# A retention and two MLP layers on one core: decay factors spread by TensorE, masks shared with ScalarE, weight conversion cut into pieces

## The chip, the cores and the metric

The kernel runs on one core of a Trainium2 chip. The metric is the device time of one execution in microseconds (us), the median of repeated runs; lower is better.

## What is computed

```
gamma[h] = 1 - 2**(-5 - h)                      # 8 heads, 2 batches, 768 steps, head size 64
state = gamma * state + outer(k[t], v[t])
y[t]  = (1/sqrt(64)) * q[t] @ state
x = y as 1536 tokens x 512
h = x @ w_in;  x = (h * sigmoid(h)) @ w_out     # layer 0: 512 -> 2048 -> 512
h = x @ w_in;  out = max(0.01 * h, h) @ w_out   # layer 1: 512 -> 2048 -> 512
```

Everything is float32 at the borders of the kernel. The weights arrive as 64-bit words of eight bytes each, which the kernel turns into float32 itself.

## The kernel before, in words

**Retention, in 12 chunks.** The sequence is cut into chunks of 128 steps, six for each of the two batches, taken in turns (`ORDER`); the loop over `j` runs over them. A chunk has a tile pair `att_t` of two halves of 512 KB: half 0 has the queries and keys with features on the rows, half 1 the values and keys with tokens on the rows. There are four such pairs, so the load of chunk j + 4 waits until chunk j has been read. The loads all stand on SP's queue (`load_att`, L104), with the first weight loads (`load_w`, L112) between them.

For chunk j TensorE does, in this order:
- `scores(j)` (L193): keys times queries, into one of two PSUM pairs
- `values(j)`: values times the masked scores `P` (L212), then the carried state times the queries (L221, not in a batch's first chunk), then the addition `u` to the state (L230, not in a batch's last chunk)

`scores(j + 1)` is issued ahead of `values(j)`. VectorE does `masked(j)` (L200: `P` = scores times mask `M`), `store_x(j)` (the output is split into a rounded part `xh`, copied by ScalarE at L255, and a remainder `xl`, L256) and `state(j)` (L241, L243). GpSimd (POOL) does `queries(j)` (L169: queries times the decay factors `G`, in place), `keys(j)` (L175) and `decay(j)` (L182).

The decay factors `G` (128 rows x 512) scale the output. For the first LATE = 4 chunks VectorE multiplies the finished product by `G` (L251) inside `store_x`; from chunk 4 on POOL multiplies the queries, before `scores` may read them. `G` comes by a load of its own (L361), the sixth on SP's queue. The masks `M`, one for each of the 8 heads, are made by VectorE (L366) from one mask and a column of factors that both arrive with the small load `cs` (L344).

**Weights.** A weight tile of 128 x 512 words goes through five steps: the load into `ws` (three buffers), `words` on ScalarE (L130, L131: two activations into `r` and `u`, two buffers of each), `conv` on VectorE (L137, L141, L145, L149, four instructions in a row), and `split_w` (a rounded copy by ScalarE, L154, and the remainder by VectorE, L155). `keep_w` (L116) then stores the pair to a scratch, from which later sets of tokens fetch it. The first six weights are `early`. Weights 0 and 1 are converted within the retention (at j = 5 and j = 9), 2 and 3 right behind it.

**The MLP layers.** The 1536 tokens are three sets of 512. `up` (L269) makes one of 16 blocks of 128 hidden features for one set, 12 matmuls into PSUM bank 3 or 2 in turns; `act` (L281, L283) reads that bank twice on ScalarE, which frees it, and VectorE makes the remainder (L284, called `rest`); `down` (L297) adds the block into four banks. For sets 0 and 1 the list `ops` goes up, up, down, over and over. Each engine works its instructions in the order in which the loop over `ops` issues them: at step i the conversion (`conv`) of the weight that step i + SPLIT = i + 5 needs, then `act` of step i - 1, then `words` for step i + 6, then the remainder, then `split_w`:

```
            for w in at(i + SPLIT, is_new):
                conv(w)
            done = i and ops[i - 1][1] == 0
            if done:
                rest = act(*ops[i - 1][:1], *ops[i - 1][2:])
            for w in at(i + SPLIT + 1, is_new):
                words(w)
            if done:
                rest()
            for w in at(i + SPLIT, is_new):
                split_w(w)
```

Of the kernel before, what the change touches and what calls it, by code (L numbers as in the profile page):

```python
# [9 lines left out]
F32 = mybir.dt.float32  # L10
# [4 lines left out]
AF = mybir.ActivationFunctionType  # L15
ALU = mybir.AluOpType
# [12 lines left out]
CS = T // C  # L29
ORDER = [b * NC + c for c in range(NC) for b in range(B)]  # L30
WARM = 18
LATE = 4
LAG = 2
SPLIT = 5
FETCH = 5
# [9 lines left out]
def retention_moe_kernel(ctx: ExitStack, tc: tile.TileContext, att, w1, w2, cst, out):  # L45
# [84 lines left out]
        nc.scalar.activation(out=r.bitcast(F32), in_=t[:, :, 1].bitcast(F32), func=AF.Abs)  # L130
        nc.scalar.activation(out=u, in_=t[:, :, 0].bitcast(U32), func=AF.Copy, scale=2.0 ** -29)  # L131

    def conv(w):
        t = stage.pop(w)
        r, u = rs[w]

        nc.vector.tensor_scalar(  # L137
            out=r.bitcast(F32), in0=r.bitcast(F32), scalar1=MIN_NORMAL, scalar2=MAX_NORMAL,
            op0=ALU.max, op1=ALU.min,
        )  # L140
        nc.vector.tensor_scalar(  # L141
            out=r, in0=r, scalar1=3, scalar2=0x3FFFFFF8,
            op0=ALU.logical_shift_left, op1=ALU.bitwise_and,
        )
        nc.vector.scalar_tensor_tensor(  # L145
            out=r, in0=t[:, :, 1], scalar=-0x40000000, in1=r, op0=ALU.bitwise_and, op1=ALU.bitwise_or
        )

        nc.vector.tensor_tensor(out=r, in0=r, in1=u, op=ALU.add)  # L149

    def split_w(w):
        r = rs.pop(w)[0].bitcast(F32)
# [189 lines left out]

    with tc.manual_schedule():
        nc.scalar.dma_start(out=cs, in_=cst[:, 0:ncs])  # L344
        z = gp.tile([128, 256], BF, tag="gf", name="z")
        nc.vector.memset(z, 0.0)
        warm = bank(3)
        for i in range(WARM):
            nc.tensor.matmul(out=warm[:, 0:256], lhsT=z[:, 0:128], rhs=z, start=True, stop=True)

        z1 = gp.tile([128, 1], F32, tag="gf", name="z1")
        nc.vector.memset(z1, 0.0)
        nc.scalar.activation(out=z1, in_=z1, func=AF.Silu)

        early = [weight[i] for i in range(SPLIT + 4) if new[i]]
        load_att(0, 0)
        load_att(1, 0)
        load_att(0, 1)
        load_att(2, 0)
        load_att(1, 1)  # L360
        nc.sync.dma_start(out=G, in_=cst[:, ncs:])  # L361
        load_att(3, 0)
        load_att(2, 1)
        load_att(3, 1)
        for h in range(H):
            nc.vector.tensor_scalar(  # L366
                out=M[:, h % 2, (h // 2) * C:(h // 2) * C + C], in0=mask, scalar1=MD[:, h:h + 1],
                scalar2=None, op0=ALU.mult,
            )
        NJ = len(ORDER)  # L370
        scores(0)
        masked(0, 2)
        for j in range(NJ):
            if j + 1 < NJ:
                queries(j + 1)
                scores(j + 1)
            keys(j)
            decay(j)
            values(j)
            if j + 4 < NJ:  # L380
                load_att(j + 4, 0, 1)

            if j in (1, 3, 5, 6, 10):
                load_w(early[(1, 3, 5, 6, 10).index(j)])
            w = early[(5, 9).index(j)] if j in (5, 9) else None
            if w:
                words(w)
            if j == NJ - 2:
                words(early[2])
            if j + 1 < NJ:  # L390
                masked(j + 1)
            if w:
                conv(w)
            store_x(j)
            state(j)
            if w:
                split_w(w)
            if j in (7, 11):
                keep_w(early[(7, 11).index(j)])
        conv(early[2])  # L400
        split_w(early[2])
        words(early[3])
        load_w(early[5])
        keep_w(early[2])
        widen()

        for i, op in enumerate(ops):
            l, p, b, f = op
            if i >= len(ops) - LAST:
                break  # L410
            for w in at(i + SPLIT + 4, is_new):
                if w not in early:
                    load_w(w)
            for w in at(i + SPLIT - 1, is_new):
                if w not in early[:3]:
                    keep_w(w)
            for w in at(i + FETCH, is_old):
                fetch_w(w)
            if p == 0:
                up(l, b, f)  # L420
            else:
                for m in range(4):
                    down(m, l, b, f)
                    if f == NF - 1:
                        finish(m, l, b, f)
                free.append(gt.pop((l, b, f)))
            if not kept[i]:
                free.append(W.pop(weight[i]))
# [6 lines that stand above are left out]
                words(w)  # L435
            if done:
                rest()
            for w in at(i + SPLIT, is_new):
                split_w(w)
        for m in range(4):  # L440
            for l, p, b, f in ops[-LAST:]:
                down(m, l, b, f)
            finish(m, l, b, f)
# [47 lines left out]
```

## Time and profile before

| what | value |
|---|---|
| median of 3 runs | 587.32 us (585.93 to 587.69) |
| the profiled execution: its time, its span | 586.51 us, 584.7 us |
| TensorE busy | 570.3 us (98% of the span) |
| VectorE, ScalarE, POOL busy | 285.3 us (49%), 234.6 us (40%), 25.9 us (4%) |
| retention: first to last matmul of it | 5.12 to 52.95 us |
| mean granted TensorE clock | 0.997 |

The span is the time from the first to the last instruction of the profiled execution; 1.8 us of its own time lie around it. A share of busy time is a mean over stages: TensorE is busy almost throughout, and what it waits for lies in the first 63 us.

### The profile page before, as it was taken

The page shows a single profiled execution, that of the slowest core. Times are in us where ns is not written, and L with a number is a line of the kernel's source. Part 1 is how long each engine was busy: PE and PEld are TensorE (multiplying, and loading weights), DVE is VectorE, ACT ScalarE, POOL GpSimd, SP SyncE. Part 2 cuts the span into 40 slices and gives each one's busy share as a digit, 9 for nine tenths or more (in the row PEclk, how much of TensorE's full clock was granted, in tenths as well). Part 3 has the DMA queues.
Part 4 walks back from the last instruction along what each step waited for, and adds up shares of the span by engine and source line. Part 5 has one row for each costly group of instructions (what it writes and reads, how often), then busy time and mean ns, then how long its engine had stood idle before and what let it go on. Part 6 is the DMA issues. An engine that isn't in the chain of part 4 may idle for free.

```text
span 584.7 us, 8034 instructions
## 1 busy us (share of the span) xinstructions
PE 570.3 (98%) x3026; PEld 472.0 (81%) x3026; DVE 285.3 (49%) x477; ACT 234.6 (40%) x422; POOL 25.9 (4%) x30
## 2 busy tenths in 40 slices
PE   7899799999999999999999999999999999999997
PEld 6787688888888888888888888888888888888885
DVE  4777888888883311134975635776661111110000
ACT  1223766766663322144655434555452312213001
POOL 2860000000000000000000000000000000000000
PEclk9999899999999999999999999999999999999999
DMA  8994777777758855718598777798876965562901
GB/s 323 344 340 161 262 235 266 240 265 241 259 187 295 296 200 186 275 46 306 203 360 305 282 254 261 238 336 296 286 252 236 370 208 194 189 207 82 384 3 72
DMA packets 40071, 142.43 MB, mean 244 GB/s; under 512 B 4448, under 2 KB 4576, under 8 KB 40032
## 3 DMA queue, kind: packets, MB, share of 16 engines
q1 hardware_dynamic: 39744, 141.58, 68.4%
q8 instruction: 24, 0.39, 0.3%
q10 hardware_dynamic: 288, 0.34, 0.2%
q14 instruction: 15, 0.12, 0.1%
HBM read 105.20 MB, written 36.70 MB: 243 GB/s over the span
## 4 chain that ended last, share of the span: by engine, by line
PE 92%; DVE 3%; DMA 3%; ACT 1%; issue 0%; POOL 0%; SPq 0%; DVEq 0%; ACTq 0%; POOLq 0%
PE b L269 44%; PE p L297 22%; PE b L297 22%; DMA G<-cst_dram 1%; DMA att_t<-att_dram 1%; PE b L212 1%; PE b L221 1%; PE p L193 1%; DVE P L200 1%; POOL att_t L169 0%; SPq L104 0%; PE b L230 0%; DVE r L141 0%; DVE r L145 0%; DVE xl L256 0%
## 5 line engine op out<-in xcount | busy, mean ns | idle before, releaser
L269 PE MATMUL b<-xh,s 128*128 128x512 f32 x560 | 183.0, 392 | 3.4 <-ACT s L281 3.4
L269 PEld LDWEIGHTS b<-xh,s 128*128 128x128 f32 x560 | 106.0, 189 | 26.1 <-ACT s L281 3.8
L284 DVE TENSOR_TENSOR s<-gf,s 128x512 fp32r<-128x512 f32 x73 | 50.4, 691 | 142.0 <-ACT s L283 94.6
L269 PE MATMUL b<-xl,s 128*128 128x512 f32 x280 | 109.5, 391 | 0.0
L297 PE MATMUL b<-s,s 128*128 128x512 f32 x288 | 73.1, 389 | 0.0
L297 PE MATMUL p<-s,s 128*128 128x512 f32 x288 | 73.1, 389 | 0.0
L283 ACT ACTIVATE gf<-b 128x512 f32<-128x512 f32 x48 | 28.6, 596 | 103.0 <-PE b L269 103.0
L269 PE MATMUL b<-xh,sr 128*128 128x512 f32 x208 | 67.8, 389 | 0.0
L297 PEld LDWEIGHTS b<-s,s 128*128 128x128 f32 x288 | 54.1, 188 | 11.2
L297 PEld LDWEIGHTS p<-s,s 128*128 128x128 f32 x288 | 54.1, 188 | 11.2
L269 PEld LDWEIGHTS b<-xl,s 128*128 128x128 f32 x280 | 53.0, 189 | 10.9
L281 ACT ACTIVATE gf<-b 128x512 f32<-128x512 f32 x48 | 28.3, 590 | 62.9 <-PE b L269 62.7
L154 ACT ACTIVATE s<-r 128x512 fp32r<-128x512 f32 x46 | 29.1, 633 | 59.3 <-DVE r L149 59.3
L149 DVE CUSTOM_DVE_ANT_0 r<-r,u 128x1024 uint16<-128x1024 uint16 x64 | 44.3, 692 | 7.2
L269 PEld LDWEIGHTS b<-xh,sr 128*128 128x128 f32 x208 | 39.1, 188 | 8.1
L145 DVE SCALAR_TENSOR_TENSOR r<-ws,r 128x512 int32<-128x512 int32 x64 | 44.3, 693 | 2.2
L130 ACT ACTIVATE r<-ws 128x512 f32<-128x512 f32 x64 | 43.1, 674 | 2.0 <-DMA ws<-w_dram 2.0
L131 ACT ACTIVATE u<-ws 128x512 int32<-128x512 uint32 x64 | 43.3, 677 | 0.0
L269 PE MATMUL b<-xl,sr 128*128 128x512 f32 x104 | 40.5, 389 | 0.0
L155 DVE TENSOR_TENSOR s<-r,s 128x512 fp32r<-128x512 f32 x46 | 31.8, 690 | 16.1 <-ACT s L154 14.7
L284 DVE TENSOR_TENSOR sr<-gf,sr 128x512 fp32r<-128x512 f32 x23 | 15.9, 691 | 41.9 <-ACT sr L283 21.1
L297 PE MATMUL b<-sr,s 128*128 128x512 f32 x120 | 30.4, 389 | 0.0
(56 smaller groups left out, 557.0 us busy)
## 6 DMA issues: line engine op xcount, KB each, us to landing
s<-scr SPq DMA_DIRECT2D x71, 512.0 KB, 4.5
ws<-w_dram SPq DMA_DIRECT2D x64, 512.0 KB, 4.9
scr<-s SPq DMA_DIRECT2D x46, 512.0 KB, 3.1
sr<-scr SPq DMA_DIRECT2D x41, 512.0 KB, 4.4
att_t<-att_dram SPq DMA_DIRECT2D x24, 512.0 KB, 7.3
scr<-sr SPq DMA_DIRECT2D x18, 512.0 KB, 3.0
out_dram<-ob SPq DMA_DIRECT2D x11, 256.0 KB, 2.1
G<-cst_dram SPq DMA_DIRECT2D x1, 256.0 KB, 7.8
```

The lines of the kernel that those rows point to most:

```text
L130: nc.scalar.activation(out=r.bitcast(F32), in_=t[:, :, 1].bitcast(F32), func=AF.Abs)
L131: nc.scalar.activation(out=u, in_=t[:, :, 0].bitcast(U32), func=AF.Copy, scale=2.0 ** -29)
L145: nc.vector.scalar_tensor_tensor(out=r, in0=t[:, :, 1], scalar=-0x40000000, in1=r, op0=ALU.bitwise_and, op1=ALU.bitwise_or)
L149: nc.vector.tensor_tensor(out=r, in0=r, in1=u, op=ALU.add)
L154: nc.scalar.activation(out=t[:, 0], in_=r, func=AF.Copy)
L155: nc.vector.tensor_tensor(out=t[:, 1], in0=r, in1=t[:, 0].bitcast(F32), op=ALU.subtract)
L193: nc.tensor.matmul(out=sc[:, r, c], lhsT=kT[s, c], rhs=q[s, c], start=True, stop=True)
L269: nc.tensor.matmul(out=h, lhsT=w[:, tw, k * 128:k * 128 + 128], rhs=(xh, xl)[tx][b][:, k, :], start=(n == 0), stop=(n == 3 * NP - 1),)
L281: nc.scalar.activation(out=t, in_=h, func=AF.Silu)
L283: nc.scalar.activation(out=t, in_=h, func=AF.Prelu, alpha=0.01)
L284: return lambda: nc.vector.tensor_tensor(out=g[:, 1, :], in0=gf, in1=g[:, 0, :].bitcast(F32), op=ALU.subtract)
L297: nc.tensor.matmul(out=ys[m], lhsT=l, rhs=r, start=(f == 0 and n == 0), stop=(f == NF - 1 and n == 2),)
```

## The change

- LATE goes from 4 to 5: the output of chunk 4 is scaled by VectorE behind its products, and POOL does not multiply its queries.
- `G` is no longer loaded. Two rows of it (one for each half of the rows) come in a 4 KB load `g2` on ScalarE's queue, right behind `cs`. At j = 0, between `scores(1)` and `values(0)`, two matmuls with a row of ones (`one`) write it to all rows of a PSUM bank, and ScalarE copies that to `G`.
- Four of the eight masks are made by ScalarE.
- `conv` is two functions, `conv1` (the first two instructions) and `conv2` (the last two). For weights 0 and 1 the three pieces `conv1`, `conv2` and `split_w` stand one at each of chunks 5, 6, 7 and 8, 9, 10, each behind `state(j)`. Weight 2 is converted within chunk 11, and `words` of weight 3 stands there too.
- `split_w` and `keep_w` of weight 3 stand at step 1 of the MLP layers, behind the first activation.
- On SP's queue the load of weight 3 stands behind the last loads of the retention, and the scratch store of weight 0 a chunk later.

```diff
--- before.py
+++ after.py
@@ -29,7 +29,7 @@
 CS = T // C
 ORDER = [b * NC + c for c in range(NC) for b in range(B)]
 WARM = 18
-LATE = 4
+LATE = 5
 LAG = 2
 SPLIT = 5
 FETCH = 5
@@ -130,9 +130,8 @@
         nc.scalar.activation(out=r.bitcast(F32), in_=t[:, :, 1].bitcast(F32), func=AF.Abs)
         nc.scalar.activation(out=u, in_=t[:, :, 0].bitcast(U32), func=AF.Copy, scale=2.0 ** -29)
 
-    def conv(w):
-        t = stage.pop(w)
-        r, u = rs[w]
+    def conv1(w):
+        r = rs[w][0]
 
         nc.vector.tensor_scalar(
             out=r.bitcast(F32), in0=r.bitcast(F32), scalar1=MIN_NORMAL, scalar2=MAX_NORMAL,
@@ -142,11 +141,19 @@
             out=r, in0=r, scalar1=3, scalar2=0x3FFFFFF8,
             op0=ALU.logical_shift_left, op1=ALU.bitwise_and,
         )
+
+    def conv2(w):
+        t = stage.pop(w)
+        r, u = rs[w]
         nc.vector.scalar_tensor_tensor(
             out=r, in0=t[:, :, 1], scalar=-0x40000000, in1=r, op0=ALU.bitwise_and, op1=ALU.bitwise_or
         )
 
         nc.vector.tensor_tensor(out=r, in0=r, in1=u, op=ALU.add)
+
+    def conv(w):
+        conv1(w)
+        conv2(w)
 
     def split_w(w):
         r = rs.pop(w)[0].bitcast(F32)
@@ -342,6 +349,11 @@
 
     with tc.manual_schedule():
         nc.scalar.dma_start(out=cs, in_=cst[:, 0:ncs])
+
+        g2 = wst.tile([1, 2, NP * C], F32, tag="ws", name="g2")
+        nc.scalar.dma_start(out=g2, in_=cst[0:128:64, ncs:].unsqueeze(0))
+        one = wst.tile([1, 64], F32, tag="ws", name="one")
+        nc.gpsimd.memset(one, 1.0)
         z = gp.tile([128, 256], BF, tag="gf", name="z")
         nc.vector.memset(z, 0.0)
         warm = bank(3)
@@ -358,48 +370,56 @@
         load_att(0, 1)
         load_att(2, 0)
         load_att(1, 1)
-        nc.sync.dma_start(out=G, in_=cst[:, ncs:])
         load_att(3, 0)
         load_att(2, 1)
         load_att(3, 1)
         for h in range(H):
-            nc.vector.tensor_scalar(
-                out=M[:, h % 2, (h // 2) * C:(h // 2) * C + C], in0=mask, scalar1=MD[:, h:h + 1],
-                scalar2=None, op0=ALU.mult,
-            )
+            m = M[:, h % 2, (h // 2) * C:(h // 2) * C + C]
+            if h < H // 2:
+                nc.vector.tensor_scalar(
+                    out=m, in0=mask, scalar1=MD[:, h:h + 1], scalar2=None, op0=ALU.mult
+                )
+            else:
+                nc.scalar.activation(out=m, in_=mask, func=AF.Copy, scale=MD[:, h:h + 1])
         NJ = len(ORDER)
         scores(0)
         masked(0, 2)
+
+        piece = {5: (conv1, 0), 6: (conv2, 0), 7: (split_w, 0),
+                 8: (conv1, 1), 9: (conv2, 1), 10: (split_w, 1)}
         for j in range(NJ):
             if j + 1 < NJ:
                 queries(j + 1)
                 scores(j + 1)
+            if j == 0:
+                gb = bank(2)
+                for r in range(2):
+                    nc.tensor.matmul(
+                        out=gb[64 * r:64 * r + 64, :], lhsT=one, rhs=g2[:, r, :],
+                        start=True, stop=True,
+                    )
+                nc.scalar.activation(out=G, in_=gb, func=AF.Copy)
             keys(j)
             decay(j)
             values(j)
             if j + 4 < NJ:
                 load_att(j + 4, 0, 1)
-
-            if j in (1, 3, 5, 6, 10):
-                load_w(early[(1, 3, 5, 6, 10).index(j)])
-            w = early[(5, 9).index(j)] if j in (5, 9) else None
-            if w:
-                words(w)
-            if j == NJ - 2:
-                words(early[2])
+            if j in (1, 3, 5, 7, 10):
+                load_w(early[(1, 3, 5, 7, 10).index(j)])
+            if j in (8, 11):
+                keep_w(early[(8, 11).index(j)])
+            if j in (5, 8, 10, 11):
+                words(early[(5, 8, 10, 11).index(j)])
             if j + 1 < NJ:
                 masked(j + 1)
-            if w:
-                conv(w)
+            if j == NJ - 1:
+                conv(early[2])
             store_x(j)
             state(j)
-            if w:
-                split_w(w)
-            if j in (7, 11):
-                keep_w(early[(7, 11).index(j)])
-        conv(early[2])
+            if 5 <= j < NJ - 1:
+                step, n = piece[j]
+                step(early[n])
         split_w(early[2])
-        words(early[3])
         load_w(early[5])
         keep_w(early[2])
         widen()
@@ -412,7 +432,7 @@
                 if w not in early:
                     load_w(w)
             for w in at(i + SPLIT - 1, is_new):
-                if w not in early[:3]:
+                if w not in early[:4]:
                     keep_w(w)
             for w in at(i + FETCH, is_old):
                 fetch_w(w)
@@ -435,8 +455,12 @@
                 words(w)
             if done:
                 rest()
-            for w in at(i + SPLIT, is_new):
+
+            for w in at(i + SPLIT, is_new) if i else ():
                 split_w(w)
+            if i == 1:
+                split_w(early[3])
+                keep_w(early[3])
         for m in range(4):
             for l, p, b, f in ops[-LAST:]:
                 down(m, l, b, f)
```

How the engines' instructions move shows at three places. The first is TensorE at the start: `p` are the scores, `b` the products, up to the second chunk's `scores`. Before:

```order
L193 MATMUL p_167<-att_t 128x128 x8
L193 MATMUL p_179<-att_t 128x128 x8
L212 MATMUL b_189<-P,att_t 64x128 x8
L230 MATMUL b_190<-att_t 64x64 x8
L193 MATMUL p_216<-att_t 128x128 x8
```

And now:

```order
L200 MATMUL p_170<-att_t 128x128 x8
L200 MATMUL p_182<-att_t 128x128 x8
L397 MATMUL b_191<-g_126,one 64x512 x2
L219 MATMUL b_196<-P,att_t 64x128 x8
L237 MATMUL b_197<-att_t 64x64 x8
L200 MATMUL p_223<-att_t 128x128 x8
```

Two matmuls of 512 columns stand ahead of the first products. The second place is VectorE around the last mask multiplication of the retention, the last row of both fences (`P<-p_643` before, `P<-p_649` now), from the mask multiplication ahead of it on. Before:

```order
L200 TENSOR_TENSOR P<-p_590,M 128x1024
L137 TENSOR_SCALAR r<-r 128x512
L141 TENSOR_SCALAR r<-r 128x512
L145 SCALAR_TENSOR_TENSOR r<-ws,r 128x512
L149 ISA r<-r,u 128x1024
L256 TENSOR_TENSOR xl_93<-b_601,xh_90 128x4x128
L243 TENSOR_TENSOR st_86<-st_87,b_602 128x256
L155 TENSOR_TENSOR s_103<-r,s_103 128x512
L200 TENSOR_TENSOR P<-p_643,M 128x1024
```

And now:

```order
L207 TENSOR_TENSOR P<-p_604,M 128x1024
L263 TENSOR_TENSOR xl_93<-b_615,xh_90 128x4x128
L250 TENSOR_TENSOR st_86<-st_87,b_616 128x256
L148 SCALAR_TENSOR_TENSOR r<-ws,r 128x512
L152 ISA r<-r,u 128x1024
L207 TENSOR_TENSOR P<-p_649,M 128x1024
```

Three instructions of weight 1 have left the stretch between the two. The third place is ScalarE from the end of the retention to the first activation of the MLP (`gf<-b_724` before, `gf<-b_732` now; `s_103`, `s_104` and so on are the rounded copies of weights 1, 2 and 3). Before:

```order
L154 ACTIVATE s_103<-r 128x512
L130 ACTIVATE r<-ws 128x512
L131 ACTIVATE u<-ws 128x512
L255 ACTIVATE xh_90<-b_652 128x4x128
L255 ACTIVATE xh_90<-b_680 128x4x128
L154 ACTIVATE s_104<-r 128x512
L130 ACTIVATE r<-ws 128x512
L131 ACTIVATE u<-ws 128x512
L154 ACTIVATE s_105<-r 128x512
L281 ACTIVATE gf<-b_724 128x512
```

And now:

```order
L262 ACTIVATE xh_90<-b_658 128x4x128
L161 ACTIVATE s_103<-r 128x512
L130 ACTIVATE r<-ws 128x512
L131 ACTIVATE u<-ws 128x512
L262 ACTIVATE xh_90<-b_688 128x4x128
L161 ACTIVATE s_104<-r 128x512
L288 ACTIVATE gf<-b_732 128x512
```

The rounded copy of weight 3 no longer stands ahead of the first activation.

## Rows read from the trace of the kernel before

**Rows 1.** Timeline of TensorE: start, us, instructions, [idle before <- what ended it]

```profile
5.12 2.43 PE L193 MATMUL p<-att_t 64*128 64x128 f32 x32 [0.47 <-DMA att_t<-att_dram]
...
8.26 1.09 PE L212 MATMUL b<-P,att_t 128*64 128x128 f32 x16 [0.71 <-DVE P L200]
...
15.07 1.09 PE L212 MATMUL b<-P,att_t 128*64 128x128 f32 x16 [1.15 <-DVE P L200]
...
19.35 1.16 PE L193 MATMUL p<-att_t 64*128 64x128 f32 x16 [1.55 <-POOL att_t L169]
...
23.10 1.16 PE L193 MATMUL p<-att_t 64*128 64x128 f32 x16
...
34.94 1.16 PE L193 MATMUL p<-att_t 64*128 64x128 f32 x16 [0.52 <-POOL att_t L169]
...
50.90 1.09 PE L212 MATMUL b<-P,att_t 128*64 128x128 f32 x16 [1.30 <-DVE P L200]
...
52.95 0.50 PE L269 MATMUL b<-xh,s 128*128 128x512 f32 x1
...
62.06 0.80 PE L269 MATMUL b<-xh,s 128*128 128x512 f32 x1 [3.36 <-ACT s L281]
```

**Rows 2.** Busy time by stretch: length, PE, PEld, DVE, ACT, POOL, PEclk, DMA, GB/s

```profile
5.00:23.00 18.00, 14.23 (x240) 12.20 (x240) 13.14 (x24) 1.89 (x3) 8.67 (x9) 1.00 1.02 400
23.00:30.00 7.00, 7.00 (x120) 5.93 (x116) 5.37 (x9) 2.37 (x4) 6.69 (x8) 1.00 0.81 260
...
62.06:65.50 3.44, 3.44 (x8) 2.76 (x9) 3.23 (x6) 3.44 (x7) 0.00 (x0) 0.50 0.55 212
...
69.23:77.39 8.16, 8.16 (x37) 6.76 (x36) 6.58 (x13) 5.28 (x11) 0.00 (x0) 1.00 0.71 251
```

**Rows 3.** The chain of waits in order of time: start, us, what

```profile
3.53 7.81 DMA G<-cst_dram
...
11.47 0.70 DVE yg L251
...
13.88 1.14 DVE P L200
```

**Rows 4.** Timeline of POOL (GpSimd), two of its multiplications

```profile
8.26 1.04 POOL L175 TENSOR_TENSOR att_t<-att_t,cs 128x512 f32<-128x512 f32 x1 [7.82 <-DMA att_t<-att_dram]
...
24.42 1.39 POOL L169 TENSOR_TENSOR att_t<-att_t,G 128x512 f32<-128x512 f32 x1 [0.31 <-DMA att_t<-att_dram]
```

**Rows 5.** DMA issues, the load issued at 6.42 us: KB, us to landing

```profile
att_t<-att_dram SPq DMA_DIRECT2D x1, 512.0 KB, 11.5
```

**Rows 6.** Timeline of VectorE: masks, conversions

```profile
5.28 1.66 DVE L366 TENSOR_SCALAR M<-cs 128x128 f32<-128x128 f32 x8 [4.27 <-DMA cs<-cst_dram]
...
45.25 1.38 DVE L141 TENSOR_SCALAR r<-r 128x512 int32<-128x512 int32 x1
...
54.30 0.42 DVE L137 TENSOR_SCALAR r<-r 128x512 f32<-128x512 f32 x1
54.75 0.43 DVE L141 TENSOR_SCALAR r<-r 128x512 int32<-128x512 int32 x1
...
57.33 0.69 DVE L155 TENSOR_TENSOR s<-r,s 128x512 fp32r<-128x512 f32 x1 [0.70 <-ACT s L154]
...
62.65 0.42 DVE L137 TENSOR_SCALAR r<-r 128x512 f32<-128x512 f32 x1
```

**Rows 7.** Timeline of ScalarE, around the MLP's start and 100 us later

```profile
60.41 0.63 ACT L154 ACTIVATE s<-r 128x512 fp32r<-128x512 f32 x1 [1.98 <-DVE r L149]
...
70.46 0.68 ACT L130 ACTIVATE r<-ws 128x512 f32<-128x512 f32 x1
...
162.55 0.67 ACT L130 ACTIVATE r<-ws 128x512 f32<-128x512 f32 x1
...
170.43 0.59 ACT L281 ACTIVATE s<-b 128x512 fp32r<-128x512 f32 x1
```

**Rows 8.** Timeline of TensorE, the down step behind the ups at 170 us

```profile
175.31 1.52 PE L297 MATMUL b<-s,s 128*128 128x512 f32 x6
```

## The prediction

> **What bounds the kernel now.** I read the granted clock and the busy shares first: TensorE is busy 98% of the span, so what can be won lies in its idle times and its slow stretches. The timeline of TensorE [rows 1] shows them: the retention idles 0.71, 1.15, 1.55, 0.52 and 1.30 us, and the MLP's third `up` waits 3.36 us at 58.70, until ScalarE has emptied a PSUM bank. Behind that wait the busy-time view shows a granted clock of 0.50 [rows 2], that is 1.2 of 2.4 GHz, for 3.44 us. From 69.23 on three steps of the MLP take 8.16 us at clock 1.00 [rows 2], and no idle time follows; so whatever TensorE gains before 63 us reaches the end, unless a new wait takes it.
>
> Next the chain of waits [rows 3]: the load of `G` lands at 11.34, and VectorE, in order, holds the next mask multiplication `P` behind it until 15.02. The landings tell the rest: POOL's first multiplication starts as chunk 0's second half lands [rows 4], at 8.2; the load issued at 6.42 (chunk 4's queries) took 11.5 us [rows 5], so it landed at 17.9, and POOL's multiplication of 1.3 us stands between it and `scores(4)` at 19.35. These loads queue up, in a stream of 400 GB/s up to 23 us [rows 2], which is 1.3 for 512 KB and 0.65 for `G`.
>
> Last the MLP's start: ScalarE works the rounded copy of weight 3 at 60.41 [rows 7], and the first activation stands behind it in the queue, though its `up` was done by 55.7. That copy had waited 1.98 us for VectorE's conversion.
>
> **The change part by part**, in us from the span's start.
>
> *Masks, decays, start.* `scores(1)` ends at 7.55 [rows 1]. VectorE's eight masks take 1.66 [rows 6]; four take 0.83. ScalarE's four have no row; free is one bound, four activations of four times the columns at 0.68 each [rows 7] the other, 2.7, and even so the second half of `P(0)` is done by 8.6, which the second half of `values(0)` alone needs. So: no cost. The two decay matmuls have no row either. 16 matmuls of 128 columns take 1.02 (the last `values` and the state's products fill 50.90 to 52.95 with 32) [rows 1]; two of 512 columns, each in two passes as the trace shows every float32 matmul here, move as many columns: 1.02, or 2.05 if they do not overlap as those pairs do. I take 1.05: the shape on the output side is the same. `values(0)` then starts at 8.6 in place of 8.26, and `G`, behind a copy of about 0.6, is there at 9.3 in place of 11.34.
>
> *Retention.* `values(0)` ends at 9.75, and the chain that led from 11.47 to 15.02 [rows 3], 3.55 long, now ends at 13.3. TensorE's own work from `values(0)` to there took 5.65 before (8.26 to 15.07, less 1.15 idle [rows 1]), so from 8.6 on `values(2)` starts at 14.2 in place of 15.07 and ends at 16.9. `scores(4)` now waits for the load alone, which comes 0.65 earlier, without `G` ahead of it: 17.9 - 0.65 = 17.3, against 19.35. A chunk takes 3.75 (19.35 to 23.10). `scores(5)`: 21.05. `scores(6)` needs a load that POOL had at 24.42 and 1.39 of multiplication [rows 4]: 24.4 - 0.65 + 1.39 = 25.15, against 26.85 (23.10 + 3.75). From there TensorE's own work is the limit if the later loads follow: they wait for `values`, which come 1.7 to 2 us earlier, so the idle 0.52 ahead of `scores(8)` goes too: five chunks on, `scores(11)` starts at 43.9, `values(9)` has ended its state products at 43.3, and `values(10)` ends at 47.05. If the decay matmuls take 2.05, `scores(4)` comes at 17.85 and `scores(6)` at 25.35: 0.2 is all that costs.
>
> *The last `P`.* Behind 43.3 VectorE's queue holds the output, the state, `conv2` and then `P(11)`: 3.55 less the 0.70 of `yg` = 2.85 [rows 3], and 1.45 for the two `conv2` instructions (a conversion runs from 54.30 to 56.63, when VectorE begins to wait for ScalarE; its first two take 0.9) [rows 6]. So 47.6, an idle time of 0.55 in place of 1.30, and the MLP starts at 49.65 in place of 52.95: **-3.3**.
>
> *A collision.* One `L141` took 1.38 instead of 0.43 [rows 6], while POOL multiplied queries. The pieces now stand at chunks 5 to 9, where POOL works too. By the row, `conv1` of weight 1 can lose 0.95 ahead of `P(10)`, which has 1.6 to spare; nothing on the path. The Trainium skill, "SBUF — State Buffer", section "SBUF: two separate sides", says that VectorE and GpSimd share a pair of ports under an exclusive lock, also for VectorE instructions with two SBUF inputs, and that the loser waits out the whole instruction. By it `conv2` of weight 0, ahead of `P(8)` with 0.4 to spare, could wait up to 1.4 as well, and my estimate by that rule would be a sum smaller by up to 1.0; in these rows only `L141` shows such a stretch among the conversions. I keep the row.
>
> *The MLP's start.* Weight 2 is converted at 48.9 to 51.25, behind `xl(10)` and the remainder of weight 1; ScalarE's rounded copy of it ends at 51.9. The first `up` ends at 52.4, its two activations at 53.5, and the third `up` needs the bank at 49.65 + 5.45 = 55.1. So the idle **-3.36** goes. The half clock goes with it: the two `up`s from 62.06 to 69.23 took 7.17 in place of two thirds of 8.16, 5.44: **-1.73**. Sum on TensorE: -3.3 - 3.36 - 1.73 = -8.4.
>
> *What comes back.* The conversions run as one chain through VectorE and ScalarE, two weights a round, and it is slower than TensorE: 70.46 to 162.55 in 11 rounds [rows 7] is 8.37 a round, against 8.16. The activations stand in that chain. At 171.02 one has just emptied its bank [rows 7], which the second of the two `up`s ahead of 175.31 [rows 8] needs at 175.31 - 2.72 = 172.59: 1.57 to spare, the least of all rounds. The chain moves forward less than TensorE does: from 51.25 on VectorE does `xl(11)`, the remainder of weight 2, the conversion of weight 3, the first activation's remainder and that of weight 3, 5 us, and begins weight 4 at 56.3, against 62.65 [rows 6]: -6.35. TensorE can therefore end this stage 6.35 + 1.57 = 7.9 earlier at most, and waits 0.5 in some last rounds. Those waits of some 0.2 each are shorter than the idle 1.55 [rows 1], behind which the clock stayed at 1.00. Behind 180 no weight of this kind is left and the rest moves as it is.
>
> *Moved at no cost.* The load of weight 3 stands behind the retention's last loads; it goes out behind `values(7)`, near 36.7, its `words` come at 49, and the longest landing in these rows is 11.5 [rows 5]. The store of weight 0 has no reader for over 100 us. The multiplication by `G` for chunk 4, 0.70 on VectorE, is covered by TensorE's 3.75 a chunk. ScalarE holds `words` of weight 3 ahead of the last `xh`; the second `up` then has 0.4 to spare, the thinnest cover here.
>
> **Sum: -7.9.** From the profiled execution, 586.51, this gives 578.6; from the median of the three runs, 587.32, it gives 579.4. I predict **579.0**.
>
> **Rivals.**
> - *The loads do not follow* (10%). Behind 23 us the DMA stream thins out, to 260 GB/s [rows 2]; if chunks 8 to 11 land as before, `scores(8)` stays at 34.94, only the last `P` (0.95) and the MLP's start (5.1) remain: -6.0, 580.9. Against it: it thins out, as I read it, because `values(3)` frees its pair late, and that comes 2 us earlier.
> - *The conversions are the bound* (10%). If the chain moves only as far as the MLP's start does, 3.3, the end is at 3.3 + 1.57 = 4.9: 582.0. For it: the round of 8.37; against it: the three `conv1` and copy instructions that left the end of the retention, and the idle times around 58 to 61.
> - *The bank is still late* (8%): a wait of more than some 2 us at the third `up`, and with it the slow clock: -3.3 alone, 583.6.
> - *The change does not shorten the start: the decays come late* (2%, slower). TensorE stands still behind `scores(1)` until `g2` lands. If it lands behind all nine loads queued at the start, at 16, everything is 7.7 later than worked out, and an idle time of 8 brings the slow clock, 1.7: +1.5, 588.4. It decides at 14.5, beyond which the kernel is slower than before; up to 8 nothing is lost. Against it: `cs`, on the same queue beside the same loads, had landed when VectorE began the masks at 5.28 [rows 6], and `g2` is issued right behind it, which puts it at about 6. The Trainium skill, "DMA: Bandwidth & Descriptors", section "Queues, rings and completion order", says that a DMA engine takes the queues in turn, packet by packet; by that rule `g2` cannot fall behind the whole line, and 2% would be less.
>
> **How the numbers follow.** The forecast has 62%, with 577.8 to 580.3 of its own: the chain's start and the small waits are each uncertain by about half a us, and the reference by 0.8. Better than that has 4% (no bank wait and all of 8.4 or more, below 577.8). Something that I do not see, of either sign, has 4%. The range **577.2 to 583.0** holds the forecast and the first two rivals. Faster by over 0.3% (1.8 us, about what a measurement of this kernel can tell from no change) means below 585.5: forecast, better, the first three rivals, 94%, less 2 for the unseen: 0.92. Within 0.3%: 0.04. Slower: 0.04.
>
> **What would show it.** Right: no idle time ahead of the third `up`, a clock of 1.00 throughout from the first scores; `scores(4)` near 17.3, the last retention product at 49.7; small waits of about 0.2 at `up`s between 130 and 175, released by ScalarE. Wrong: an idle time over 1 us behind `scores(1)`; `scores(8)` later than 33.5; `up` waits from 60 on; bank waits of over 1 us in sum.

## The result and the profile after

| | before | after |
|---|---|---|
| median of 4 runs each, run beside each other | 586.62 us (585.45 to 587.69) | 578.17 us (577.92 to 579.30) |
| the profiled execution: its time, its span | 586.51 us, 584.7 us | 579.30 us, 577.5 us |
| TensorE busy | 570.3 us (98%) | 570.0 us (99%) |
| first `up` begins | 52.95 | 50.69 |
| TensorE's last matmul ends | 580.75 | 573.80 |
| mean granted clock | 0.997 | 1.000 |

The ratio of after to before is 0.986, with a 95% interval of 0.9835 to 0.9886: 8.4 us less, against a forecast of 579.0. The profiled execution is the slowest of the four, and its TensorE ends 580.75 - 573.80 = 6.95 earlier. The last rows of TensorE, before and after:

```profile
579.23 1.52 PE L297 MATMUL p<-s,s 128*128 128x512 f32 x6
```
```profile
572.28 1.52 PE L304 MATMUL p<-s,s 128*128 128x512 f32 x6
```

The timeline of TensorE after (start us, us, engine line, operation, out<-in, count, idle time before and what ended it; L219 is the `values` product, L200 `scores`, L397 the decay matmuls, L276 `up`), to be set beside [rows 1]:

```profile
7.56 1.07 PE L397 MATMUL b<-g,one 1*64 1x512 f32 x4
8.56 1.09 PE L219 MATMUL b<-P,att_t 128*64 128x128 f32 x16
...
13.86 1.09 PE L219 MATMUL b<-P,att_t 128*64 128x128 f32 x16
...
17.29 1.16 PE L200 MATMUL p<-att_t 64*128 64x128 f32 x16 [0.69 <-DMA att_t<-att_dram]
...
25.15 1.16 PE L200 MATMUL p<-att_t 64*128 64x128 f32 x16 [0.16 <-POOL att_t L176]
...
32.65 1.16 PE L200 MATMUL p<-att_t 64*128 64x128 f32 x16
...
41.22 1.16 PE L200 MATMUL p<-att_t 64*128 64x128 f32 x16 [0.81 <-POOL att_t L176]
...
48.64 1.09 PE L219 MATMUL b<-P,att_t 128*64 128x128 f32 x16 [0.46 <-DVE P L207]
...
50.69 0.50 PE L276 MATMUL b<-xh,s 128*128 128x512 f32 x1
...
56.03 0.62 PE L276 MATMUL b<-xh,s 128*128 128x512 f32 x2
```

Up to `scores(8)` at 32.65 each number lies within 0.35 of the forecast. The odd one is 41.22: `scores(10)` waited 0.81, which the forecast did not have. The third `up` (second of the pair of matmuls at 56.03) starts without an idle time, where before it waited 3.36. The windows of after (stretch and length, busy time and instructions of PE, PEld, DVE, ACT, POOL, then granted clock, DMA share, GB/s), from the first `up` to 66 us and to the end of the stage in which weights are converted (the start of the 47th `up` or `down`), show a clock of 1.00 where [rows 2] has 0.50:

```profile
50.69:66.00 15.31, 15.31 (x69) 12.68 (x68) 14.27 (x25) 11.07 (x22) 0.00 (x0) 1.00 0.84 275
66.00:176.52 110.52, 110.52 (x486) 90.79 (x485) 91.11 (x157) 71.12 (x131) 0.00 (x0) 1.00 0.69 242
```

What was given back shows in the waits of TensorE's weight loads between 50 and 178 (engine, tile and line, what they waited for, us in sum, times, longest):

```profile
PEld b L276 <- ACT s L288: 0.6, 2, 0.3
PEld b L276 <- ACT sr L288: 0.3, 1, 0.3
```

Three waits for the bank that an activation (L288) empties, ahead of the weight loads at 148.77, 157.13 and 165.49, 0.9 us in sum. A weight load begins some 0.2 us ahead of its matmul here, so the matmuls lose less: the pairs there take 0.74, 0.79 and 0.77 in place of 0.62, which is 0.4 in sum (the first of them, TensorE after):

```profile
148.53 0.74 PE L276 MATMUL b<-xh,s 128*128 128x512 f32 x2
```

So the 6.95 are 52.95 - 50.69 = 2.26 from the start, and 4.70 from the conversion stage, which takes 125.83 in place of 130.53: 3.36 of the wait and 1.73 of the slow clock, less 0.4 of bank waits. The window of that stage before:

```profile
52.95:183.48 130.53, 127.17 (x555) 104.86 (x554) 106.05 (x182) 82.95 (x151) 0.00 (x0) 0.99 0.68 236
```

### The profile page after: what moved, and what is told of

Same layout as the page of the kernel before. It is cut to its first block, busy times and chain, and to the rows that moved or that the text cites. A ratio compares the mean times of both kernels' runs of the same rounds, so it can differ in the third digit from the quotient of the medians.

```text
span 577.5 us, 8037 instructions
## 1 busy us (share of the span) xinstructions
PE 570.0 (99%) x3030; PEld 470.8 (82%) x3030; DVE 285.5 (49%) x474; ACT 236.3 (41%) x427; POOL 25.3 (4%) x30
## 4 chain that ended last, share of the span: by engine, by line
PE 94%; DMA 3%; DVE 1%; POOL 1%; ACT 0%; issue 0%; SPq 0%; DVEq 0%; POOLq 0%; ACTq 0%
PE b L276 45%; PE p L304 23%; PE b L304 23%; DMA att_t<-att_dram 3%; PE b L219 1%; PE b L228 1%; PE p L200 1%; POOL att_t L176 1%; DVE P L207 0%; ACT xh L262 0%; DVE xl L263 0%; PE b L397 0%; DVE yg L258 0%; DVE r L152 0%; DVE r L148 0%
## 5 line engine op out<-in xcount | busy, mean ns | idle before, releaser
L276 PE MATMUL b<-xh,s 128*128 128x512 f32 x560 | 181.9, 390 | 0.0
L276 PEld LDWEIGHTS b<-xh,s 128*128 128x128 f32 x560 | 105.1, 188 | 22.5 <-ACT s L288 0.3
L276 PE MATMUL b<-xl,s 128*128 128x512 f32 x280 | 108.9, 389 | 0.0
L276 PE MATMUL b<-xh,sr 128*128 128x512 f32 x208 | 68.0, 390 | 0.0
L276 PEld LDWEIGHTS b<-xl,s 128*128 128x128 f32 x280 | 52.5, 188 | 10.8
L288 ACT ACTIVATE gf<-b 128x512 f32<-128x512 f32 x48 | 28.2, 588 | 60.1 <-PE b L276 60.1
L276 PEld LDWEIGHTS b<-xh,sr 128*128 128x128 f32 x208 | 39.0, 188 | 8.4 <-ACT s L288 0.3
L276 PE MATMUL b<-xl,sr 128*128 128x512 f32 x104 | 40.5, 389 | 0.0
```

The costliest lines, as they stand in the source:

```text
L276: nc.tensor.matmul(out=h, lhsT=w[:, tw, k * 128:k * 128 + 128], rhs=(xh, xl)[tx][b][:, k, :], start=(n == 0), stop=(n == 3 * NP - 1),)
L288: nc.scalar.activation(out=t, in_=h, func=AF.Silu)
```

## The experiments

The leading theory: TensorE gains from the earlier start, from the wait at the third `up` and from the clock, and its end is then capped by the chain of conversions, which can give up its 1.57 us of room and no more. The rivals: the start alone did it; the bank waits have another cause; the decays or the masks cost TensorE time.

**The split back in its old place (e1).** After, but weight 3's remainder again ahead of the first activation.

```diff
-                if w not in early[:4]:
+                if w not in early[:3]:
...
-            for w in at(i + SPLIT, is_new) if i else ():
+            for w in at(i + SPLIT, is_new):
                 split_w(w)
-            if i == 1:
-                split_w(early[3])
-                keep_w(early[3])
```

> The changed kernel with one part undone: the split of weight 3 stands ahead of the first activation again, as before. My theory: what ends the long wait is that the conversions come earlier, not the place of this split. The copy of weight 3 comes near 56.1, the first activation ends at 57.7 where the third up wants its bank at 56.1: a wait of 1.6 us, the clock stays at 1.00, and the chain of conversions comes about 1.1 later, so +1.1 in the end, near 579.3. Rival: the place of this split was the wait; then 3.36 of idle time and the slow clock's 1.73 come back, +5.1, near 583.3.

Measured: 579.46, 0.9883 [0.9859, 0.9906]. The third `up` waits again, but only 1.01, and the clock stays at 1.00 (timeline and windows of TensorE):

```profile
56.98 0.50 PE L276 MATMUL b<-xh,s 128*128 128x512 f32 x1 [1.01 <-ACT s L288]
```
```profile
57.00:62.00 5.00, 5.00 (x22) 4.16 (x23) 4.66 (x9) 4.65 (x9) 0.00 (x0) 1.00 0.65 238
```

With the pieces moved, the split's old place costs 1.01 at the bank; by the medians it costs 1.3, though the two intervals overlap.

**The split alone (e2).** Before, with the lines marked - in e1's diff in place of those marked +.

> The kernel before with one part of the change alone: the split and the store of weight 3 stand behind the first activation. My theory: the wait at the third up shrinks from 3.36 to about 0.8 us and the clock does not fall, 4.3 us on TensorE at 70 us; but the chain of conversions comes only 0.4 earlier and had 1.57 to spare, so TensorE waits for banks between 100 and 175 us and the end is only 2.0 earlier, near 584.6. Rival: nothing is given back, -4.3 to -5.1, near 582.

Measured: 583.46, 0.9943 [0.9928, 0.9957], a gain of 3.1 by the medians where 2.0 was expected. The wait shrinks from 3.36 to 0.76 and the slow clock is gone, 4.3 us together, 4.5 with a start that came 0.14 earlier; but TensorE's end moves by 2.39 only. The rest is given back to the chain (timeline of TensorE; waits of its weight loads, 60 to 182 us):

```profile
59.32 0.50 PE L269 MATMUL b<-xh,s 128*128 128x512 f32 x1 [0.76 <-ACT s L281]
```
```profile
PEld b L269 <- ACT s L281: 2.5, 7, 0.7
PEld b L269 <- ACT sr L281: 0.3, 1, 0.3
```

**The start alone (e3).** Before, with `g2`, the decay matmuls, `LATE = 5` and the masks of the change, and nothing else of it. The edit is cut to its core:

```diff
-LATE = 4
+LATE = 5
...
+        nc.scalar.dma_start(out=g2, in_=cst[0:128:64, ncs:].unsqueeze(0))
...
-        nc.sync.dma_start(out=G, in_=cst[:, ncs:])
...
+                nc.scalar.activation(out=m, in_=mask, func=AF.Copy, scale=MD[:, h:h + 1])
...
+                    nc.tensor.matmul(
```

> The kernel before with the start of the change alone (decays by TensorE, fifth chunk scaled behind its products, half the masks by ScalarE). My theory: scores of chunk 4 near 17.3, the MLP starts about 2.0 earlier (near 50.9), and the wait of 3.36 with its slow clock stays as it was, since the conversions move with the retention: -2.0, near 584.6. Rival: the later loads set the pace again and nothing is left of it at the MLP's start: 0.

Measured: 584.68, 0.9974 [0.9962, 0.9985], as expected. The first `up` of the profiled execution does not come near 50.9 but at 51.88: `scores(4)` is in time at 17.23, but later in the retention TensorE waits 0.41, 0.53 and 0.18 (at 33.03 and 41.38 for POOL, at 34.72 for `P`) where the theory had nothing. The wait at the third `up` (3.39) and the slow clock behind it stay (timeline and windows):

```profile
61.00 0.50 PE L269 MATMUL b<-xh,s 128*128 128x512 f32 x1 [3.39 <-ACT s L281]
```
```profile
62.25:65.66 3.41, 3.41 (x9) 2.67 (x8) 3.14 (x6) 2.55 (x6) 0.00 (x0) 0.50 0.59 205
```

**All but the start (e4)**, after with e3's edit undone (`LATE = 4`, `G` loaded, all masks by VectorE), and **the pieces alone (e7)**, which undoes e1's part as well.

```diff
-LATE = 5
+LATE = 4
...
-        g2 = wst.tile([1, 2, NP * C], F32, tag="ws", name="g2")
...
+        nc.sync.dma_start(out=G, in_=cst[:, ncs:])
...
-            if h < H // 2:
+            if True:
```

> The changed kernel with the start undone (decays loaded, four chunks scaled behind, all masks by VectorE); pieces and split stay. My theory: -0.9 at the MLP's start against before, no wait at the third up (-5.1), and 0.4 given back in bank waits near the end of the conversions: -5.6, near 581.0. Rival: the start is worth nothing once the pieces are in, and this kernel is as fast as the changed one, 578.2.

> The kernel before with the pieces alone (conversions in pieces, weight 2 within the last chunk, words of weight 3 there; the split of weight 3 stays ahead of the first activation, the start is the old one). My theory: -0.9 at the MLP's start, a wait of about 1.6 at the third up at full clock in place of 3.36 and the slow clock, and the chain decides the end: -4.5 against before, near 582.1. Rival: without the split's new place the long wait stays: -0.9, near 585.7.

Measured: e4 580.08, 0.9893 [0.987, 0.9915], between the two expectations and nearer the theory's; e7 581.44, 0.9915 [0.9893, 0.9937], where the theory had it. In e7 the third `up` waits 1.27 at 59.06, again at clock 1.00. The pieces are the largest single part: about 5 us alone.

e4 and e7 are the same program up to the MLP's first activation, and yet the first `up` comes 1.21 apart (TensorE, e4, then e7):

```profile
50.81 0.50 PE L276 MATMUL b<-xh,s 128*128 128x512 f32 x1
```
```profile
52.02 0.50 PE L276 MATMUL b<-xh,s 128*128 128x512 f32 x1
```

In e7 `scores(10)` waits 0.73, in e4 it does not wait. So the first `up` of a single profiled execution is known to about 1 us only, and what the start is worth is better taken from the medians: 1.9, both for e3 against before and for after against e4.

**A longer chain (e5).** After, with the clamp of `conv1` done twice in the 14 conversions of one half of layer 0's weights, about 0.4 us each.

```diff
         r = rs[w][0]
+        if w[0] == 0 and w[1] == 1 and w not in early:
+            nc.vector.tensor_scalar(
+                out=r.bitcast(F32), in0=r.bitcast(F32), scalar1=MIN_NORMAL, scalar2=MAX_NORMAL,
+                op0=ALU.max, op1=ALU.min,
+            )
```

> The changed kernel with one VectorE instruction done twice (the clamp, 0.45 us) in each conversion of a first-layer down weight from the third on: 14 more instructions, 6.3 us of VectorE. My theory: the chain of conversions is the limit by the end of this stage (0.05 us to spare at the tightest bank), so nearly all of it reaches the end: TensorE waits for banks, +5 to +6 us, near 583.8. Rival: VectorE is busy only half of the span and TensorE is the bound: 0, near 578.2.

Measured: 583.68, 0.9954 [0.9938, 0.9969]. VectorE is idle for a sixth of this stage in after (busy 14.27 + 91.11 of 125.83), and yet 14 instructions of 0.42 on it cost 5.5. The windows of the conversion stage, e5, and the waits of its matmuls:

```profile
49.96:181.29 131.33, 128.01 (x555) 103.04 (x554) 111.37 (x195) 81.93 (x151) 0.00 (x0) 1.00 0.67 233
```
```profile
PE b L281 <- ACT s L293: 2.5, 7, 0.4
PE b L281 <- ACT sr L293: 0.9, 2, 0.5
```

The stage takes 131.33 in place of 125.83, and nine `up`s wait for the bank, 3.4 us in sum. So the chain sets the end.

**The split later (e8).** After, with every remainder of the MLP's new weights a step later, behind the activation.

```diff
-            for w in at(i + SPLIT - 1, is_new):
-                if w not in early[:4]:
-                    keep_w(w)
...
-            for w in at(i + SPLIT, is_new) if i else ():
-                split_w(w)
-            if i == 1:
-                split_w(early[3])
-                keep_w(early[3])
+            for w in at(i + SPLIT - 1, is_new):
+                if w not in early[:3]:
+                    split_w(w)
+                    keep_w(w)
```

> The changed kernel with each split in the MLP one step later, so that VectorE converts the next weight while ScalarE copies this one (0.70 idle a round goes). My theory: a round of the chain falls from 8.37 to about 7.7, below TensorE's 8.16, the room ahead of the banks no longer shrinks, and the 0.4 of bank waits go: -0.4, which the time hardly shows but the timeline does. Rival: the room shrinks as before, since something other than that wait sets the round.

Measured: 577.92 (577.82 to 578.06), 0.9855 [0.983, 0.988], which cannot be told from after; no kernel tried beats after measurably. The bank waits are gone, and the stage takes 125.25 (windows of e8):

```profile
49.92:175.17 125.25, 125.25 (x555) 103.74 (x553) 102.60 (x180) 84.05 (x150) 0.00 (x0) 1.00 0.76 253
```

The expected round was wrong. `words` begin at 62.86 and, 12 rounds on, at 162.70 (ScalarE's timeline), 8.32 a round. The split that moved back now holds the buffers that `words` needs (waits of ScalarE in e8, 50 to 178 us):

```profile
62.86 0.67 ACT L130 ACTIVATE r<-ws 128x512 f32<-128x512 f32 x1 [0.64 <-DVE s L162]
...
162.70 0.67 ACT L130 ACTIVATE r<-ws 128x512 f32<-128x512 f32 x1 [1.96 <-DVE s L162]
```
```profile
ACT r L130 <- DVE s L162: 20.8, 18, 2.0
```

**The last mask first (e9).** e8, with the last `P` ahead of the rest of VectorE's queue, weight 2's load a chunk later, and the `words` of weight 3 behind the last `xh`.

```diff
-            if j in (1, 3, 5, 7, 10):
-                load_w(early[(1, 3, 5, 7, 10).index(j)])
+            if j in (1, 3, 6, 7, 10):
+                load_w(early[(1, 3, 6, 7, 10).index(j)])
...
-            if j == NJ - 1:
-                conv(early[2])
+            if j == NJ - 2:
+                conv2(early[1])
             store_x(j)
             state(j)
...
+            if j == NJ - 1:
+                words(early[3])
+                conv(early[2])
```

> The kernel with the later splits, and three moves more: the last mask multiplication of the retention ahead of the second half of weight 1's conversion, the last remainder ahead of weight 2's conversion, and the load of weight 2 a chunk later. My theory: the idle 0.5 to 0.8 ahead of the last values goes and no new wait over 0.3 takes its place, the scores of chunk 10 no longer wait for their load; about 1.0 less than the changed kernel, near 577.2. Rival: VectorE is then late for the third up's bank, and the wait moves there: no gain, 578.

Measured: 578.25, 0.9857 [0.9843, 0.9872], no gain; which of the moves took back the other's is not shown. The idle time ahead of the last `values` is gone, and a new one stands ahead of the fourth `up` (TensorE, e9):

```profile
47.46 1.09 PE L219 MATMUL b<-P,att_t 128*64 128x128 f32 x16
...
58.53 0.50 PE L276 MATMUL b<-xh,s 128*128 128x512 f32 x1 [0.52 <-ACT s L288]
```

**The decay matmuls twice (e6).** After, with the two matmuls issued a second time, onto the same values.

```diff
-                for r in range(2):
+                for r in (0, 1, 0, 1):
```

> The changed kernel with the two decay matmuls done twice, about 1.0 us more of TensorE ahead of the first products. My theory: the scores of chunk 4 wait for their load anyway (0.69 us idle), so they come 0.3 to 0.4 later at most and the end 0 to 0.3 later. Rival: TensorE's work at the start is on the path: +1.0.

Measured: 578.72, 0.9872 [0.9848, 0.9895]; the time alone fits both expectations. The trace decides: the second pair adds 0.86 on TensorE, and `scores(4)` comes at 17.29 as in after (TensorE, e6):

```profile
7.61 1.93 PE L397 MATMUL b<-g,one 1*64 1x512 f32 x8
...
17.29 1.16 PE L200 MATMUL p<-att_t 64*128 64x128 f32 x16
...
49.84 0.50 PE L276 MATMUL b<-xh,s 128*128 128x512 f32 x1
```

**The three parts of the start, one undone at a time:** `G` loaded (e10), four chunks scaled (e11), all masks by VectorE (e12).

```diff
+        nc.sync.dma_start(out=G, in_=cst[:, ncs:])
...
-                gb = bank(2)
```
```diff
-LATE = 5
+LATE = 4
```
```diff
-            if h < H // 2:
+            if True:
```

> The changed kernel with the decay factors loaded again as 256 KB on SP's queue, in place of the two matmuls; five chunks scaled behind, masks shared. My theory: every later load lands 0.65 later, scores of chunk 4 near 17.9 and of chunk 6 near 25.8: +0.7 of the start's 1.9. Rival: all of the start's gain comes from this, +1.9; or none, 0.

> The changed kernel with four chunks scaled behind their products in place of five, so that POOL multiplies the queries of chunk 4 ahead of its scores. My theory: scores of chunk 4 near 18.5 in place of 17.3, of chunk 6 near 26.0 in place of 25.15: +0.9. Rival: the load of chunk 6 sets the pace in both, 0.

> The changed kernel with all eight masks by VectorE. My theory: the first products wait for the load and for the decay matmuls, which end at 8.6, where the first half of the first mask multiplication ends at 7.5 either way: 0. Rival: VectorE's start is on the path: +0.8.

Measured: e10 579.61, 0.988 [0.9865, 0.9894]; e11 579.22, 0.9874 [0.9858, 0.9891]; e12 578.51, 0.9861 [0.9846, 0.9875]. `scores(4)` came at 17.75, 18.26 and 17.07, in after at 17.29. The intervals of all three overlap that of after, so none of these costs is settled by time alone. The timelines show the places (TensorE, e10, where the mask multiplication `P` is late again; then e11, where POOL's multiplication again stands ahead of `scores(4)`):

```profile
15.09 1.09 PE L219 MATMUL b<-P,att_t 128*64 128x128 f32 x16 [1.10 <-DVE P L207]
```
```profile
18.26 1.16 PE L200 MATMUL p<-att_t 64*128 64x128 f32 x16 [1.56 <-POOL att_t L176]
```

**One rule for the end.** The prediction capped the gain at what the chain moves forward plus its room of 1.57. The chain's start is VectorE's first conversion instruction of weight 4; before it stood at 62.65 [rows 6]. Two of these rows (VectorE; the first from after, the second from e6):

```profile
57.35 0.42 DVE L136 TENSOR_SCALAR r<-r 128x512 f32<-128x512 f32 x1
```
```profile
56.27 0.42 DVE L136 TENSOR_SCALAR r<-r 128x512 f32<-128x512 f32 x1
```

| kernel | first `up` | weight 4 at | cap: 62.65 less that, plus 1.57 | TensorE's end, earlier than 580.75 by |
|---|---|---|---|---|
| e6 decays twice | 49.84 | 56.27 | 7.95 | 8.07 |
| e12 masks by VectorE | 50.34 | 56.88 | 7.34 | 7.50 |
| after | 50.69 | 57.35 | 6.87 | 6.95 |
| e4 all but the start | 50.81 | 57.47 | 6.75 | 6.82 |
| e1 split back | 50.23 | 57.57 | 6.65 | 6.61 |
| e11 four scaled | 51.07 | 57.63 | 6.59 | 6.72 |
| e10 `G` loaded | 51.20 | 57.84 | 6.38 | 6.47 |
| e7 pieces alone | 52.02 | 59.65 | 4.57 | 4.58 |
| e2 split alone | 52.81 | 61.56 | 2.66 | 2.39 |
| e3 start alone | 51.88 | 61.59 | 2.63 | 1.04 |

In nine of the ten the end lies within 0.3 of the cap: e1 starts earlier than after and ends later, as its chain does. Only e3, whose wait and slow clock hold TensorE back, does not reach it. The table is weaker evidence than it looks, for in eight of the nine the plain sum of what TensorE gained (start, wait, clock) lies only 0.1 to 0.4 above the end too, and in e7 no weight load waits for a bank at all. The kernels that tell the cap from the plain sum are e2 (sum 4.5, cap 2.66, end 2.39) and e5. The three kernels that change the chain itself (e5) or its order (e8, e9) are outside this rule.

## Why the prediction was right

**Masks, decays, start.** Right. The decay matmuls took 1.07 where 1.05 was taken, `values(0)` began at 8.56 (8.6). They waited for nothing, so `g2` had landed by 7.56; the row of its landing is not in the trace. The rival of the late decays fell with that. ScalarE's four masks took 1.28, within the bounds of 0 and 2.7, and e12 shows no time that they save or cost beyond the noise.

**Retention.** Right to `scores(8)`, and with it the rival that the loads do not follow falls as a whole: 32.65, not 34.94 [rows 1]. But an idle time of 0.81 came back at `scores(10)`. POOL began chunk 10's queries at 39.90 in after and at 37.59 in e6, whose retention issues the same loads. (The profile puts POOL's wait there in after down to a state product, L228, that ends at 39.79; that multiplication reads nothing of it, and the landing falls at the same time: issued at 32.15, 7.6 later. In e6 it is issued at 32.02.) The DMA views of the two (the one issue between 32.1 and 32.3, and the one between 31.6 and 32.2: count, KB, us from issue to landing), after, then e6:

```profile
att_t<-att_dram SPq DMA_DIRECT2D x1, 512.0 KB, 7.6
```
```profile
att_t<-att_dram SPq DMA_DIRECT2D x1, 512.0 KB, 5.4
```

This is the step that failed, "`scores(11)` starts at 43.9": 44.98 in after's profiled execution, 43.78 in e6. It took 1.04 of the term of -3.3 for the start there (50.69 against 49.65), while e5, e6 and e8 begin at 49.96, 49.84 and 49.91. The prediction read before's idle 0.52 at `scores(8)` as something that earlier loads remove. The runs show it as a matter of the execution: with the old start, e2, e4 and e7 have no idle time there (34.20, 33.84 and 34.25); with the new one, in whole or in part, e1, e3, e9, e11 and e12 wait 0.41 to 0.79 there. So of the 2.29 between 34.94 and 32.65, 0.7 to 1.1 lies between executions of the old start too: that part is luck, and not the change. Why a load takes longer in one execution than in another was not tried.

**The last `P`.** An idle time of 0.46 (e6: 0.81) where 0.55 was forecast. Right in place, and in size as far as executions agree.

**A collision.** `conv1` of weight 1 lost 0.92 beside two of POOL's multiplications (VectorE, then POOL, after), and nothing on the path waited for it:

```profile
41.40 1.05 DVE L136 TENSOR_SCALAR r<-r 128x512 f32<-128x512 f32 x1
42.49 0.72 DVE L140 TENSOR_SCALAR r<-r 128x512 int32<-128x512 int32 x1
```
```profile
41.13 1.04 POOL L182 TENSOR_TENSOR att_t<-att_t,cs 128x512 f32<-128x512 f32 x1
42.13 0.80 POOL L189 TENSOR_TENSOR st<-st,cs 128x256 f32<-128x256 f32 x1
```

`conv2` of weight 0, ahead of `P(8)`, took 0.74 and 0.69 at 33.72 and 34.50 in after; POOL happened to run no multiplication of keys or queries over it, only the end of `decay` (33.30 to 33.91). In e6 and e8 POOL's multiplication of the queries lay over it (in e6 from 33.89 to 35.60): its second instruction, at 34.51 and 34.57, took 1.64 in both in place of 0.69, and with the first `conv2` lost 1.14 and 1.26. So the loss of up to 1.4 that the prediction named and set aside for the row of `L141` does come; it is its price, "a sum smaller by up to 1.0", that did not. `scores(9)` ended at 37.36 in e6 and at 37.32 in e8, and `values(8)` behind it began at 37.37 and 37.40: less than 0.1 was lost on TensorE, so the 0.4 to spare was put too low. Here the forecast held by more room than it had counted.

**The MLP's start.** Right in both terms: no idle time ahead of the third `up`, -3.36, and no slow clock, -1.73. e1 and e7 show what the two parts do: with the pieces alone the wait is 1.27, with pieces and start 1.01, and only the split's new place takes it to nothing. Each of them, and the split alone too, already ends the slow clock. The rival of the late bank fell.

**What comes back.** Right in mechanism and in size: forecast 0.5, measured 0.4 beside the later start. Weight 4 begins 5.30 earlier in after and 6.38 in e6, where 6.35 was forecast; the cap worked out for e6's start, 7.95, is the 7.9 of the sum, and its TensorE ends 8.07 earlier. After's median, 8.4 below that of before, lies near that; its profiled execution was the late one. The rival that the conversions are the bound at 4.9 fell; its mechanism stands, since the chain is the bound in after too, only with a chain that moved as far as was worked out. The three parts alone (e2, e3 and e7: 3.1, 1.9 and 4.8 by the medians) exceed the whole by 1.4, which fits a cap and two parts that remove the same wait, but is no more than their intervals leave open. The time of after does not show the term either: the interval of its gain, 6.7 to 9.7, holds 7.9 as well as the 8.4 that the sum has without it, and the medians give 8.4. What shows it is the three waits in after, e2 and e5. And e8, without the cap's waits, which are worth 0.6 on the stage, gained nothing in time that could be told.

**Moved at no cost.** No idle time stands ahead of the second `up`, for which the last cover was 0.4, nor ahead of any other before the three at the bank. Right.

## What to carry to other kernels

Where a producing chain runs slightly slower than TensorE, with a little room at its last round, the gain from removing idle time ahead of it is capped by how far the chain's own start moves, plus that room: look up the least room before adding up idle times. An instruction on an engine that is busy only part of the time can still cost nearly its whole length (in e5 14 of 0.42 us, 5.9 in sum, cost 5.5), so test it by lengthening it, as e5 does. And where loads land at different times in each execution, compare medians before calling a wait a part of the kernel. When a wait is removed, count what the clock behind it returns as a term of its own.

## What the runs showed of the hardware

- Behind TensorE's waits of 0.76, 1.01, 1.27 (e2, e1, e7) and 1.55 ([rows 1]) the granted clock stayed at 1.00; behind 3.36 and 3.39 (before, e3) it fell to 0.50, that is 1.2 of 2.4 GHz. A wait need not go altogether to bring its second cost to nothing: in e2 the 0.76 that remain leave the clock whole.
- A VectorE instruction with two inputs in SBUF is stretched by POOL's as well, not only `conv1`. The remainder `xl` of the first chunks is such a one; VectorE, then POOL, after:

```profile
11.16 1.18 DVE L263 TENSOR_TENSOR xl<-yg,xh 128x512 fp32r<-128x512 f32 x1 [0.70 <-ACT xh L262]
...
15.10 1.39 DVE L263 TENSOR_TENSOR xl<-yg,xh 128x512 fp32r<-128x512 f32 x1 [0.70 <-ACT xh L262]
...
19.25 0.69 DVE L263 TENSOR_TENSOR xl<-yg,xh 128x512 fp32r<-128x512 f32 x1 [0.70 <-ACT xh L262]
```
```profile
10.75 1.04 POOL L182 TENSOR_TENSOR att_t<-att_t,cs 128x512 f32<-128x512 f32 x1 [1.41 <-DMA att_t<-att_dram]
...
14.90 1.04 POOL L182 TENSOR_TENSOR att_t<-att_t,cs 128x512 f32<-128x512 f32 x1
```

  It takes 0.69 with POOL idle when it begins, and 1.18 and 1.39 begun within a multiplication of POOL's: it ends 0.55 behind POOL's both times, as if it had waited for that one's end; so does `conv2`'s second instruction in e6, 1.64 long, which ends at 36.15 behind POOL's 35.60. The lock that the Trainium skill describes ("SBUF — State Buffer", section "SBUF: two separate sides"), by which the loser waits out the other's whole instruction, agrees with these rows.
- Loads of 512 KB, issued at the same place of the retention, took 5.4 us to land in one kernel's execution (e6) and 7.6 in another's (after), though the two differ in two matmuls only; in e4 and e7, which are the same program up to there, the one issued at 33.34 took 6.2 and the one at 33.74 took 7.4.
